# A fixed order on all engines for the attention half of an attention and MoE kernel

## The chip, the cores and the metric

The kernel runs on one core of a Trainium2 chip. The metric is the device time of one launch in microseconds (us). A core has five engines that run side by side, each working through its own queue: TensorE (PE, matrix multiplies into PSUM), VectorE (DVE), ScalarE (ACT), GpSimd (POOL, which has no access to PSUM) and SyncE (SP, which here issues the DMAs). Data lies in SBUF; PSUM has eight banks of 128 x 512 float32.

## What is computed

```
attn = softmax(causal(q @ k.T / 8))          # 2 batches x 12 heads, 448 x 64
x    = (attn @ v)                            # reshaped to 896 tokens x 768
g    = s * relu(x @ w_in)**2 + b             # 768 -> 2048
x2   = g @ w_out                             # 2048 -> 768
y    = sigmoid(x2 @ w_gate) * (x2 @ w_val)   # 768 -> 1536, twice
out  = y @ w_out2                            # 1536 -> 768
```

The divisor of the softmax is the sum of the row's exponentials plus 1e-9. The weights arrive as float64.

## The kernel before

Two heads of one batch form a pair, so there are 12 pairs, and tokens are columns: every activation is kept transposed. In the matrix products after the attention weight and activation are both split into a high and a low part, and three matmuls (`mm3`, line 104) per 128 x 128 block are added in one PSUM bank, 448 columns (one batch half) at a time. A weight block of 128 output columns is loaded as 64-bit words and turned into its two parts by `split_weights` (line 62): one DMA, an absolute value on ACT (line 70), two `tensor_scalar` (71, 74) and two `scalar_tensor_tensor` (78, 81) on DVE, the high part on ACT (87) and the low part on DVE (88). Five such blocks can be held ready (`bufs=AHEAD + 1`).

The attention of a pair has these parts. `scores` (207) makes the scores of one chunk of 128 queries for both heads, and `softmax` (199) takes each from PSUM with one DVE instruction that adds the mask, scales, and finds the row's maximum (202), then one ACT exponential that also sums the row (205). `scores3` does the last 64 queries of both heads at once. `sums` makes the reciprocals of the seven sums on DVE, copies six of them out to rows on POOL (242), and multiplies the last query chunk's probabilities by its own reciprocal on POOL (244). `transposed` (254) turns the probabilities in four groups of four 128 x 128 transposes, each group in one PSUM bank and copied out by ACT or DVE. `rows_of_sums` turns the copied reciprocals too (three transposes, line 283, one ACT copy). `values` (287) multiplies with v into one bank, and `output` (299) multiplies that by the reciprocals on DVE (304) and makes the high and the low part of x on POOL (305, 306).

The rounds run over i = 0 to 13: in round i the scores of pair i are made, the transposes of pair i - 1, and the values of pair i - 2. The first product's first four weight blocks (`AHEAD = 4`) are worked on early for the first batch: from round 8 on `fill` puts half a block (9 matmuls) in each round, two halves in rounds 12 and 13, and the rest behind the loop; then the second batch half of the four blocks follows. Seven PSUM banks go round for all of this, and one is kept for the values.

What sets the order: only PE is held to the order of the code (`manual_schedule(engines={PE})`). For DVE, ACT, POOL and SP a planner orders the instructions by priorities and costs of its own; the splits of the weight blocks are among them, and run early. After the loop the planner orders everything.

Of the kernel before, what the change touches and what calls it, by code (L numbers as in the profile page):

```python
# [15 lines left out]
P = 128  # L16
# [6 lines left out]
def body(ctx: ExitStack, tc: tile.TileContext, qk, vp, w_in, w_out, s, b, w_gate, w_val, w_out2, outT):  # L23
# [8 lines left out]
    AHEAD = 4  # L32
# [11 lines left out]
    wp = ctx.enter_context(tc.tile_pool(name="wp", bufs=AHEAD + 1))  # L44
# [17 lines left out]
    def split_weights(src, n):  # L62

        raw = wp.tile([P, U * P, 2], U32, tag="raw", name="raw", bufs=2)
        nn = n * P
        nc.sync.dma_start(out=raw[:, :nn], in_=src)
# [3 lines left out]
        nc.scalar.activation(out=f32(tt), in_=f32(high), func=AF.Abs)  # L70
        nc.vector.tensor_scalar(  # L71
            out=f32(tt), in0=f32(tt), scalar1=F64_TINY, scalar2=F64_HUGE, op0=ALU.max, op1=ALU.min,
        )
        nc.vector.tensor_scalar(  # L74
            out=tt, in0=tt, scalar1=0x07FFFFFF, scalar2=3,
            op0=ALU.bitwise_and, op1=ALU.logical_shift_left,
        )
        nc.vector.scalar_tensor_tensor(  # L78
            out=tt, in0=low, scalar=29, in1=tt, op0=ALU.logical_shift_right, op1=ALU.bitwise_or,
        )  # L80
        nc.vector.scalar_tensor_tensor(  # L81
            out=tt, in0=high, scalar=0xC0000000, in1=tt, op0=ALU.bitwise_and, op1=ALU.bitwise_or,
        )
        hi = wp.tile([P, U, P], F32R, tag="whi", name="whi")
        lo = wp.tile([P, U, P], F32R, tag="wlo", name="wlo")
        hif, lof = hi.rearrange("p k m -> p (k m)"), lo.rearrange("p k m -> p (k m)")
        nc.scalar.activation(out=hif[:, :nn], in_=f32(tt), func=AF.Copy)  # L87
        nc.vector.tensor_tensor(out=lof[:, :nn], in0=f32(tt), in1=f32(hif[:, :nn]), op=ALU.subtract)  # L88
        return hi, lo
# [16 lines left out]
    def product(src, K, x, tag):  # L106

        acc = [bank(f"acc{h}", tag) for h in range(B)]
        for unit in units(src, K):
            for h in range(B):  # L110
                mm3(acc[h], unit, K, x, h)
        return acc
# [30 lines left out]
    def first_evac(f, h, acc):  # L143
        gh, gl = at_g(f, h)
        g = ev.tile([P, S], F32, tag="e", name="g")
        nc.scalar.activation(out=g, in_=acc[:, :S], func=AF.Relu)
        nc.scalar.activation(out=g, in_=g, func=AF.Square)
        nc.vector.tensor_scalar(out=g, in0=g, scalar1=s_sb, scalar2=b_sb, op0=ALU.mult, op1=ALU.add)
        nc.scalar.activation(out=gh, in_=g, func=AF.Copy)
        lo = nc.gpsimd if f < AHEAD else nc.vector  # L150
        lo.tensor_tensor(out=gl, in0=g, in1=f32(gh), op=ALU.subtract)


    with tc.tile_pool(name="at", bufs=2) as at:
# [17 lines left out]

        all_rs = [at.tile([P, S], F32, name=f"rs{n}", bufs=1) for n in range(2)]
        for rs in all_rs:
            nc.gpsimd.memset(rs[:, NF * P:], 1.0)

# [5 lines left out]
        def load(i):  # L182

            if i >= N:
                return
            bb, hp = pairs[i]
            t = st[i]
            t["qk"] = at.tile([P, W], F32, tag="qk", name="qk", bufs=3)
            if i == 0:
                for c in range(NF):  # L190
                    both = [x[:, :2 * NF * P].rearrange("p (a b) -> p a b", a=2) for x in (t["qk"], qk[bb, hp])]
                    nc.sync.dma_start(out=both[0][:, :, c * P:(c + 1) * P], in_=both[1][:, :, c * P:(c + 1) * P])
                nc.sync.dma_start(out=t["qk"][:, 2 * NF * P:], in_=qk[bb, hp, :, 2 * NF * P:])
            else:
                nc.sync.dma_start(out=t["qk"], in_=qk[bb, hp])
            t["vt"] = at.tile([P, NQ, 2, D], F32, tag="vt", name="vt", bufs=4)
            nc.sync.dma_start(out=t["vt"], in_=vp[bb, hp])
# [9 lines left out]
        def scores(i, c):  # L207

            t = st[i]
            if "pt" not in t:  # L210
                t["pt"] = at.tile([P, 2, PO[-1] + NF * P], F32, tag="pt", name="pt", bufs=2)
                t["m"] = at.tile([P, NF * 2 + 1], F32, tag="m", name="m", bufs=3)
                t["l"] = at.tile([P, NF * 2 + 1], F32, tag="l", name="l", bufs=3)
# [9 lines left out]
        def scores3(i):  # L223

            t = st[i]
            sc = bank("sc3", "w")
            k0 = NF * P
            nc.tensor.matmul(sc[:, :S], t["qk"][:, k0 + S:], t["qk"][:, k0:k0 + S], start=True, stop=True)  # L228
            t["pt3"] = at.tile([P, S], F32, tag="pt3", name="pt3", bufs=2)
            cl = slice(NF * 2, NF * 2 + 1)  # L230
            softmax(t["pt3"], sc[:, :S], mask3, t["m"][:, cl], t["l"][:, cl])

        def sums(i):

            t = st[i]
            r = t["r"] = at.tile([P, NF * 2 + 1], F32, tag="r", name="r", bufs=3)
# [3 lines left out]
            t["rb"] = at.tile([P, NF, 2, D], F32, tag="rb", name="rb", bufs=2)  # L240
            by_chunk = r[:, :NF * 2].rearrange("p (j c o) -> p c j o", j=2, o=1)
            nc.gpsimd.tensor_copy(out=t["rb"], in_=by_chunk.to_broadcast([P, NF, 2, D]))

            nc.gpsimd.tensor_scalar(
                out=t["pt3"], in0=t["pt3"], scalar1=r[:, NF * 2:], scalar2=None, op0=ALU.mult,
            )
# [7 lines left out]
        def transposed(i):  # L254
# [16 lines left out]
            for j, copy in ((0, act), (1, dve)):  # L271
# [4 lines left out]
            put([pt3[:, k0:k0 + P] for k0 in (0, P, 2 * P, S - P)], ptT[:, :, :, NF * P:], act, "p (b a q) -> p a b q")  # L276

        def rows_of_sums(i):

            t = st[i]  # L280
            rs = bank("rs", "w")
            for c in range(NF):
                nc.tensor.transpose(rs[:, c * P:(c + 1) * P], t["rb"][:, c].rearrange("p j d -> p (j d)"), ident)  # L283
            t["rs"] = all_rs[i % 2]
            act(t["rs"][:, :NF * P], rs[:, :NF * P])
# [13 lines left out]
        def output(i):  # L299

            bb, hp = pairs[i]
            t = st[i]
            x = at.tile([P, S], F32, tag="x", name="x", bufs=2)
            nc.vector.tensor_tensor(out=x, in0=t["po"][:, :S], in1=t["rs"], op=ALU.mult)
            nc.gpsimd.tensor_copy(out=x_hi[:, hp, cols(bb)], in_=x)
            nc.gpsimd.tensor_tensor(
                out=x_lo[:, hp, cols(bb)], in0=x, in1=f32(x_hi[:, hp, cols(bb)]), op=ALU.subtract,
            )
            t.clear()

        ahead = []

        def fill(f, h, k0, k1):

            if k0 == 0:
                ahead_acc.append(bank("acc", "w"))
            wh, wl, _, _ = ahead[f][0]
            mm3(ahead_acc[-1], (wh[:, k0:k1], wl[:, k0:k1], k0, k1), KC, at_x(x_hi, x_lo), h)
            if k1 == KC:
                first_evac(f, h, ahead_acc[-1])  # L320

        ahead_acc = []

        early = [(f, k) for f in range(AHEAD) for k in range(0, KC, 3)]
        FIRST = NP + 2
        SPLIT = (5, 7, 9, 10)
        with tc.manual_schedule(engines={mybir.EngineType.PE}):
            load(0)
            load(1)
            for i in range(N + 2):  # L330
                load(i + 2)
# [3 lines left out]
                if i in SPLIT:  # L335
                    ahead.append(list(units(w_in[SPLIT.index(i)], KC)))
# [3 lines left out]
                if i >= 2:  # L340
                    values(i - 2)
                    output(i - 2)
                if i < N:
                    scores(i, 2 if i == 0 else 0)
                    scores3(i)
                    sums(i)
                if 1 <= i <= N:
                    transposed(i - 1)
                    rows_of_sums(i - 1)
                if i >= FIRST:  # L350
                    for _ in range(1 if i < N else 2):
                        f, k = early.pop(0)
                        fill(f, 0, k, k + 3)
            for f, k in early:
                fill(f, 0, k, k + 3)
            for f in range(AHEAD):
                fill(f, 1, 0, KC)

# [6 lines left out]
    for f in range(AHEAD, NF1):  # L365
        acc = product(w_in[f], KC, at_x(x_hi, x_lo), TAGS[f % 2])
# [11 lines left out]
    for d in range(KC - 1):  # L378
        acc = product(w_out[d], NF1, at_g, TAGS[d % 2])
# [24 lines left out]
    for d in range(KC):  # L404
        acc = product(w_out2[d], NF2, at_x(y_hi, y_lo), TAGS[d % 2])
# [56 lines left out]
```

## Time and profile before

| | |
|---|---|
| median of 3 runs | 596.69 us (596.21 to 597.32) |
| the profiled execution | 597.58 us, of which the trace spans 595.8 |
| PE busy | 583.8 us, 3036 matmuls |
| DVE busy | 382.3 us |
| ACT busy | 276.0 us |
| POOL busy | 59.4 us |
| values of the last pair issued on PE | up to 106.87 us |

A matmul's row is longer than the step from one matmul to the next, since they are pipelined; steps between starts are what counts on PE. DVE and ACT rows overlap their successor by 0.06 to 0.1 us.

### The profile page before, as it was taken

Reading aid. Unit: us, or ns where it says so; the run is one execution under the profiler, and the core shown is the slowest. Engines: PE = TensorE matmul, PEld = TensorE weight load, DVE = VectorE, ACT = ScalarE, POOL = GpSimd, SP = SyncE. Lnnn points to the kernel's source line nnn. Section 1 sums busy time; section 2 is a strip of 40 time slices with the busy share of each in tenths; the row PEclk is TensorE's granted clock in tenths of the full one; section 3 lists DMA queues with packets and bytes.
Section 4 is the critical chain, followed back from the end, with each engine's and each line's share of the span. In section 5 each row is a group of like instructions: output and inputs, shape, how many; then the busy total and the mean of one; then the engine's idle time right before and its main releaser. Section 6 shows DMA issues by size and latency. Waiting matters only on the chain.

```text
span 595.8 us, 7911 instructions
## 1 busy us (share of the span) xinstructions
PE 583.8 (98%) x3036; PEld 516.8 (87%) x3036; DVE 382.3 (64%) x682; ACT 276.0 (46%) x526; POOL 59.4 (10%) x69
## 2 busy tenths in 40 slices
PE   6999999999999999999999999999999999999997
PEld 3666677899999999999999999999999999999996
DVE  4699964399977776566664766666666666655000
ACT  6789786566766642332332433333333333332100
POOL 2455564320000000000000000000000000000000
PEclk9899999999999999999999999999999999999999
DMA  8366620024342332433341433333333333541000
GB/s 262 132 212 204 201 79 1 1 106 161 114 133 90 98 98 88 126 113 98 113 153 54 134 131 106 107 106 107 107 106 107 106 107 106 172 143 43 33 31 32
DMA packets 16407, 65.80 MB, mean 110 GB/s; under 512 B 2032, under 2 KB 4464, under 8 KB 16368
## 3 DMA queue, kind: packets, MB, share of 16 engines
q1 hardware_dynamic: 16368, 65.28, 33.6%
q8 instruction: 24, 0.39, 0.3%
q14 instruction: 15, 0.12, 0.1%
HBM read 62.52 MB, written 2.75 MB: 110 GB/s over the span
## 4 chain that ended last, share of the span: by engine, by line
PE 92%; DMA 3%; DVE 2%; ACT 2%; SPq 0%; issue 0%; POOL 0%; ACTq 0%; POOLq 0%
PE acc L104 83%; PE po L294 3%; PE tp L267 2%; PE sc L218 2%; DMA raw<-in_w_in 2%; PE sc L228 1%; ACT pt L205 1%; DMA qk<-in_qk 1%; DVE pt L202 1%; PE rs L283 0%; ACT wt L70 0%; DVE ptT L252 0%; DVE wlo L88 0%; DVE wt L81 0%; DVE wt L78 0%
## 5 line engine op out<-in xcount | busy, mean ns | idle before, releaser
L104 PE MATMUL acc<-x_hi,whi 128*128 128x448 f32 x480 | 175.8, 366 | 0.0
L104 PE MATMUL acc<-x_hi,wlo 128*128 128x448 f32 x480 | 175.3, 365 | 0.0
L104 PE MATMUL acc<-x_lo,whi 128*128 128x448 f32 x480 | 175.3, 365 | 0.0
L88 DVE TENSOR_TENSOR wlo<-wt,whi 128x768 fp32r<-128x768 f32 (+1 forms) x70 | 66.2, 945 | 80.7 <-ACT whi L87 80.6
L87 ACT ACTIVATE whi<-wt 128x768 fp32r<-128x768 f32 (+1 forms) x70 | 57.9, 827 | 121.7 <-PE acc L104 121.7
L104 PEld LDWEIGHTS acc<-x_hi,whi 128*128 128x128 f32 x480 | 90.2, 188 | 7.1
L104 PEld LDWEIGHTS acc<-x_hi,wlo 128*128 128x128 f32 x480 | 90.1, 188 | 7.1
L104 PEld LDWEIGHTS acc<-x_lo,whi 128*128 128x128 f32 x480 | 90.2, 188 | 7.1
L70 ACT ACTIVATE wt<-raw 128x768 f32<-128x768 f32 (+1 forms) x70 | 61.8, 883 | 35.0 <-DVE wlo L88 31.2
L81 DVE SCALAR_TENSOR_TENSOR wt<-raw,wt 128x768 uint32<-128x768 uint32 (+1 forms) x70 | 67.8, 968 | 1.1
L78 DVE SCALAR_TENSOR_TENSOR wt<-raw,wt 128x768 uint32<-128x768 uint32 (+1 forms) x70 | 65.8, 940 | 2.1
L71 DVE TENSOR_SCALAR wt<-wt 128x768 f32<-128x768 f32 (+1 forms) x70 | 39.4, 562 | 34.2 <-ACT wt L70 34.0
L104 PE MATMUL acc<-gb_hi,whi 128*128 128x448 f32 x144 | 52.6, 365 | 0.0
L104 PE MATMUL acc<-gb_hi,wlo 128*128 128x448 f32 x144 | 52.6, 365 | 0.0
L104 PE MATMUL acc<-y_hi,whi 128*128 128x448 f32 x144 | 52.6, 365 | 0.0
L104 PE MATMUL acc<-y_lo,whi 128*128 128x448 f32 x144 | 52.6, 365 | 0.0
L104 PE MATMUL acc<-y_hi,wlo 128*128 128x448 f32 x144 | 52.6, 365 | 0.0
L104 PE MATMUL acc<-gb_lo,whi 128*128 128x448 f32 x144 | 52.6, 365 | 0.0
L205 ACT ACTIVATE pt<-pt,m 128x128 f32<-128x128 f32 (+3 forms) x84 | 43.8, 524 | 13.9 <-DVE m L202 13.8
L202 DVE CUSTOM_DVE_ANT_0 pt<-sc,mask 128x128 f32<-128x128 f32 (+3 forms) x84 | 33.6, 444 | 15.9 <-PE sc L218 13.9
L74 DVE TENSOR_SCALAR wt<-wt 128x768 uint32<-128x768 uint32 (+1 forms) x70 | 40.0, 572 | 1.8
L395 ACT ACTIVATE y_hi<-y 128x448 fp32r<-128x448 f32 x24 | 13.9, 579 | 56.9 <-DVE y L394 56.9
(60 smaller groups left out, 673.7 us busy)
## 6 DMA issues: line engine op xcount, KB each, us to landing
raw<-in_w_out SPq DMA_DIRECT2D x18, 768.0 KB, 4.4
raw<-in_w_in SPq DMA_DIRECT2D x16, 768.0 KB, 4.4
raw<-in_w_gate SPq DMA_DIRECT2D x12, 768.0 KB, 4.3
raw<-in_w_val SPq DMA_DIRECT2D x12, 768.0 KB, 4.3
raw<-in_w_out SPq DMA_DIRECT2D x12, 640.0 KB, 4.0
qk<-in_qk SPq DMA_DIRECT2D x11, 480.0 KB, 5.1
vt<-in_vp SPq DMA_DIRECT2D x12, 256.0 KB, 3.8
outT<-ot SPq DMA_DIRECT2D x12, 224.0 KB, 1.9
```

The source lines that it names most:

```text
L70: nc.scalar.activation(out=f32(tt), in_=f32(high), func=AF.Abs)
L71: nc.vector.tensor_scalar(out=f32(tt), in0=f32(tt), scalar1=F64_TINY, scalar2=F64_HUGE, op0=ALU.max, op1=ALU.min,)
L74: nc.vector.tensor_scalar(out=tt, in0=tt, scalar1=0x07FFFFFF, scalar2=3, op0=ALU.bitwise_and, op1=ALU.logical_shift_left,)
L78: nc.vector.scalar_tensor_tensor(out=tt, in0=low, scalar=29, in1=tt, op0=ALU.logical_shift_right, op1=ALU.bitwise_or,)
L81: nc.vector.scalar_tensor_tensor(out=tt, in0=high, scalar=0xC0000000, in1=tt, op0=ALU.bitwise_and, op1=ALU.bitwise_or,)
L87: nc.scalar.activation(out=hif[:, :nn], in_=f32(tt), func=AF.Copy)
L88: nc.vector.tensor_tensor(out=lof[:, :nn], in0=f32(tt), in1=f32(hif[:, :nn]), op=ALU.subtract)
L104: nc.tensor.matmul(acc[:, :S], w[:, k - k0], m, start=k == 0 and i == 0, stop=k == K - 1 and i == 2)
L202: nc.vector.tensor_tensor_reduce(out=pc, in0=sc, in1=mk, scale=-SCALE, scalar=3.0e38, op0=ALU.add, op1=ALU.min, accum_out=m,)
L205: nc.scalar.activation(out=pc, in_=pc, func=AF.Exp, scale=-1.0, bias=m, accum_out=l)
L294: nc.tensor.matmul(po[j * D:(j + 1) * D, k * P:S], t["vt"][:, k, j], t["ptT"][:, j, k, k * P:], start=k == 0, stop=k == NQ - 1,)
L395: nc.scalar.activation(out=yh, in_=y, func=AF.Copy)
```

## The change

All engines are held to the code's order within the attention (`manual_schedule()` without a list). The transposes of a pair move one round further back (two rounds behind its scores), the values to three rounds behind; there are now 15 rounds. All seven probability tiles of a pair are multiplied by their reciprocals on POOL, in the round after the scores, by an instruction with two operations (times the reciprocal, times 1.0). So the transposes and the copy of the reciprocals go, the multiplication behind the values goes, and the two parts of x are taken straight from PSUM, the high one by ACT and the low one by DVE. Of the four copies behind the transposes DVE now does two and ACT two. `AHEAD` is 2: two blocks are worked on early, in rounds 12 and 13, and three more are split in the attention (`READY = 3`). The splitting of a block is cut into seven steps (load; Abs; two `tensor_scalar`; first, second `scalar_tensor_tensor`; high part; low part) that are put in by hand: one in round 2, two in each round from 3 on (one at the round's head, one ahead of the values), and more in rounds 12 to 14. Loads of v are issued later than those of q and k. Core of the diff:

```diff
-    AHEAD = 4
+    AHEAD = 2
+    READY = 3
...
-        lo = nc.gpsimd if f < AHEAD else nc.vector
-        lo.tensor_tensor(out=gl, in0=g, in1=f32(gh), op=ALU.subtract)
+        nc.vector.tensor_tensor(out=gl, in0=g, in1=f32(gh), op=ALU.subtract)
...
+        def divide(i):
+            t = st[i]
+            r = at.tile([P, NF * 2 + 1], F32, tag="r", name="r", bufs=4)
             nc.vector.tensor_scalar(out=r, in0=t["l"], scalar1=1e-9, scalar2=None, op0=ALU.add)
             nc.vector.reciprocal(out=r, in_=r)
...
+            for n, p in [
+                (j * NF + c, t["pt"][:, j, PO[c]:PO[c] + (c + 1) * P]) for c in (0, 2, 1) for j in range(2)
+            ] + [(NF * 2, t["pt3"])]:
+                nc.gpsimd.tensor_scalar(
+                    out=p, in0=p, scalar1=r[:, n:n + 1], scalar2=1.0, op0=ALU.mult, op1=ALU.mult,
+                )
...
+        def output_hi(i):
+            bb, hp = pairs[i]
+            act(x_hi[:, hp, cols(bb)], st[i]["po"][:, :S])
+        def output_lo(i):
+            bb, hp = pairs[i]
+            nc.vector.tensor_tensor(
+                out=x_lo[:, hp, cols(bb)], in0=st[i]["po"][:, :S], in1=f32(x_hi[:, hp, cols(bb)]), op=ALU.subtract,
+            )
...
-        with tc.manual_schedule(engines={mybir.EngineType.PE}):
+        with tc.manual_schedule():
+            load_qk(0)
+            load_qk(1)
+            for i in range(N + 3):
+                load_qk(i + 2)
+                load_v(i - 1)
...
+                on(i - 1, divide)
+                if i >= 2:
+                    step()
                 if i < N:
                     for c in (0, 1) if i == 0 else (2, 1):
                         scores(i, c)
+                if i >= 3:
+                    step()
+                on(i - 3, values)
+                on(i - 3, output_hi)
                 if i < N:
                     scores(i, 2 if i == 0 else 0)
+                on(i - 3, output_lo)
+                on(i, scores3)
+                tail = i >= N
+                if i == N:
+                    fill(0, 0, 0, KC)
+                    step(3)
+                t = turned(i - 2) if 0 <= i - 2 < N else iter(())
+                next(t, None)          # first group of transposes, ACT copy
+                on(i, softmax3)
+                next(t, None)          # three more groups: DVE, ACT, DVE copies
+                if i == N + 1:
+                    fill(1, 0, 0, KC)
+                if tail:
+                    step(4)
             for f in range(AHEAD):
                 fill(f, 1, 0, KC)
+                step(5)
```

The comments behind the two `next` lines are added here.

## Rows read from the trace of the kernel before

**Rows 1.** The page's busy time by engine, and two windows (busy by engine, clock).

```profile
PE 583.8 (98%) x3036; PEld 516.8 (87%) x3036; DVE 382.3 (64%) x682; ACT 276.0 (46%) x526; POOL 59.4 (10%) x69
...
20.00:70.00 50.00, 47.71 (x334) 32.48 (x331) 48.13 (x146) 46.12 (x132) 26.86 (x27) 1.00 0.58 181
...
106.87:595.00 488.13, 485.45 (x2398) 449.51 (x2394) 305.19 (x431) 192.49 (x289) 8.78 (x8) 1.00 0.31 102
```

**Rows 2.** PE in order of time, one round (start, length), and behind the last values.

```profile
80.32 1.35 PE L218 MATMUL sc<-qk 64*128 64x384 f32 x8
81.60 1.95 PE L294 MATMUL po<-ptT,vt 128*64 128x448 f32 x16
83.48 0.49 PE L218 MATMUL sc<-qk 64*128 64x128 f32 x4
...
84.75 1.91 PE L267 MATMUL tp<-ident,pt 128*128 128x128 f32 x16
86.50 0.49 PE L283 MATMUL rs<-ident,rb 128*128 128x128 f32 x3
...
106.87 0.47 PE L104 MATMUL acc<-x_hi,whi 128*128 128x448 f32 x1
```

**Rows 3.** DVE in order of time: single instructions of the attention.

```profile
18.52 0.56 DVE L202 CUSTOM_DVE_ANT_0 pt<-sc,mask 128x384 f32<-128x384 f32 x1 [4.23 <-PE sc L218]
...
66.06 0.95 DVE L88 TENSOR_TENSOR wlo<-wt,whi 128x768 fp32r<-128x768 f32 x1
...
79.52 0.17 DVE L237 TENSOR_SCALAR r<-l 128x7 f32<-128x7 f32 x1 [0.72 <-ACT pt L205]
...
89.69 0.56 DVE L202 CUSTOM_DVE_ANT_0 pt<-sc,mask 128x384 f32<-128x384 f32 x1 [2.43 <-PE sc L218]
...
92.12 0.62 DVE L304 TENSOR_TENSOR x<-po,rs 128x448 f32<-128x448 f32 x1 [0.69 <-ACT pt L205]
...
93.49 0.62 DVE L202 CUSTOM_DVE_ANT_0 pt<-sc,mask 128x448 f32<-128x448 f32 x1 [0.33 <-POOL x_hi L305]
...
94.69 0.69 DVE L252 COPY ptT<-tp 128x512 f32<-128x512 f32 x1 [0.57 <-PE tp L267]
```

**Rows 4.** ACT: the page's group of all exponentials, then rows in order of time.

```profile
L205 ACT ACTIVATE pt<-pt,m 128x128 f32<-128x128 f32 (+3 forms) x84 | 43.8, 524 | 13.9 <-DVE m L202 13.8
```

**Rows 5.** ACT in order of time: single instructions of the attention.

```profile
9.04 0.67 ACT L205 ACTIVATE pt<-pt,m 128x448 f32<-128x448 f32 x1 [0.67 <-DVE m L202]
...
59.91 0.95 ACT L70 ACTIVATE wt<-raw 128x768 f32<-128x768 f32 x1
...
78.26 0.58 ACT L249 ACTIVATE ptT<-tp 128x512 f32<-128x512 f32 x1
78.74 0.66 ACT L205 ACTIVATE pt<-pt,m 128x448 f32<-128x448 f32 x1
...
90.30 0.61 ACT L205 ACTIVATE pt<-pt,m 128x384 f32<-128x384 f32 x1 [2.30 <-DVE m L202]
...
92.40 0.18 ACT L205 ACTIVATION_READ_ACCUMULATOR pt<-pt,m 128x1 f32 x1
```

**Rows 6.** Evacuation of an early block: ACT, DVE and POOL in order of time.

```profile
105.09 0.55 ACT L146 ACTIVATE g<-acc 128x448 f32<-128x448 f32 x1 [3.06 <-PE acc L104]
...
106.28 0.51 DVE L148 TENSOR_SCALAR g<-g,s_sb,b_sb 128x448 f32<-128x448 f32 x1 [4.97 <-ACT g L147]
...
107.48 1.15 POOL L151 TENSOR_TENSOR ga_lo<-g,ga_hi 128x448 fp32r<-128x448 f32 x1 [4.93 <-ACT ga_hi L149]
```

**Rows 7.** Windows at the start: busy PE, PEld, DVE, ACT, POOL, granted clock, DMA.

```profile
13.00:16.00 3.00, 0.38 (x3) 0.38 (x4) 0.68 (x3) 2.06 (x7) 1.91 (x2) 1.00 1.01 415
...
18.00:19.00 1.00, 1.00 (x6) 0.34 (x2) 0.47 (x1) 0.00 (x0) 0.00 (x0) 0.50 0.07 31
```

**Rows 8.** POOL groups of 0 to 110 us: busy us, mean ns of one.

```profile
L244 POOL TENSOR_SCALAR pt<-pt,r 128x448 f32<-128x448 f32 x12 | 17.6, 1463 | 0.0
...
L305 POOL CAST x_hi<-x 128x448 fp32r<-128x448 f32 x12 | 6.7, 557 | 15.4 <-DVE x L304 15.3
```

More of the change, by code (lines that the diff above doesn't have):

```diff
@@ L77, in split_weights @@
         )
+        yield
         nc.vector.scalar_tensor_tensor(
@@ L87, in split_weights @@
         nc.scalar.activation(out=hif[:, :nn], in_=f32(tt), func=AF.Copy)
+        yield
         nc.vector.tensor_tensor(out=lof[:, :nn], in0=f32(tt), in1=f32(hif[:, :nn]), op=ALU.subtract)
-        return hi, lo
+        out += [hi, lo]
+    def split_weights(src, n):
+        out = []
+        for _ in split_steps(load_words(src, n), n, out):
+            pass
+        return out
     def units(src, K):
@@ L104, in mm3, with product @@
                 nc.tensor.matmul(acc[:, :S], w[:, k - k0], m, start=k == 0 and i == 0, stop=k == K - 1 and i == 2)
-    def product(src, K, x, tag):
+    def product(parts, K, x, tag):
         acc = [bank(f"acc{h}", tag) for h in range(B)]
-        for unit in units(src, K):
+        for unit in parts:
             for h in range(B):
@@ L180, in body, with load_qk @@
         st = [{} for _ in pairs]
-        def load(i):
+        def load_qk(i):
             if i >= N:
@@ L311, in body @@
-        ahead = []
+            act(x_hi[:, hp, cols(bb)], st[i]["po"][:, :S])
[3 more added lines that the diff above has]
+                out=x_lo[:, hp, cols(bb)], in0=st[i]["po"][:, :S], in1=f32(x_hi[:, hp, cols(bb)]), op=ALU.subtract,
+            )
+            st[i].clear()
+        split = [[] for _ in range(AHEAD + READY)]
+        acc = {}
         def fill(f, h, k0, k1):
             if k0 == 0:
-                ahead_acc.append(bank("acc", "w"))
-            wh, wl, _, _ = ahead[f][0]
-            mm3(ahead_acc[-1], (wh[:, k0:k1], wl[:, k0:k1], k0, k1), KC, at_x(x_hi, x_lo), h)
+                acc[f] = bank("acc", "w")
+            wh, wl = split[f]
+            mm3(acc[f], (wh[:, k0:k1], wl[:, k0:k1], k0, k1), KC, at_x(x_hi, x_lo), h)
@@ L319, in fill, with splits @@
             if k1 == KC:
[L320 to L326, printed above, removed]
-        with tc.manual_schedule(engines={mybir.EngineType.PE}):
[L328 to L331, printed above, removed]
+                first_evac(f, h, acc[f])
+        def splits():
+            for f in range(AHEAD + READY):
+                raw = load_words(w_in[f], KC)
+                yield
+                yield from split_steps(raw, KC, split[f])
+                yield
@@ L332, in body, with step, on @@
+        steps = splits()
+        def step(n=1):
+            for _ in range(n):
+                next(steps, None)
+        def on(i, *what):
+            if 0 <= i < N:
+                for w in what:
+                    w(i)
+        with tc.manual_schedule():
[4 more added lines that the diff above has]
+                load_v(i - 1)
                 if i == 0:
@@ L339, in body @@
                         scores(i, c)
-                if i >= 2:
-                    values(i - 2)
-                    output(i - 2)
+                if i >= 3:
+                    step()
+                on(i - 3, values)
+                on(i - 3, output_hi)
                 if i < N:
                     scores(i, 2 if i == 0 else 0)
[L345 to L355, printed above, removed]
+                on(i - 3, output_lo)
[12 more added lines that the diff above has]
+                    step(4)
             for f in range(AHEAD):
                 fill(f, 1, 0, KC)
+                step(5)
+            for _ in steps:
+                pass
     gb = ctx.enter_context(tc.tile_pool(name="gb", bufs=1))
@@ L365, in body @@
     for f in range(AHEAD, NF1):
-        acc = product(w_in[f], KC, at_x(x_hi, x_lo), TAGS[f % 2])
+        ready = [(*split[f], 0, KC)] if f < AHEAD + READY else units(w_in[f], KC)
+        acc = product(ready, KC, at_x(x_hi, x_lo), TAGS[f % 2])
         for h in range(B):
```

80 lines of the change are left out of this document (30 added, 50 removed).

## The prediction

> **What bounds the kernel now.** First the page's busy times and the windows. From 106.87 us to the end PE works without a gap at full clock, 2398 matmuls in 485.45 us, 0.203 us each [rows 1]. The matmuls there are a fixed amount that the change doesn't touch, so a time saved or lost ahead of it passes through one to one, and the sum below is only about when PE gets into this stream. Between 20 and 70 us DVE is busy 48.13 of 50 us and ACT 46.12: the splits of seven weight blocks lie on DVE beside the softmax, and PE waits [rows 1]. From round 8 on the early blocks fill PE.
>
> PE's order shows one round: 80.32 to 86.50 us is 6.18 us for scores (1.28 and 1.27), values (1.88) and 16 transposes (1.75); the reciprocals' transposes come behind that [rows 2].
>
> Before, 54 matmuls of the early blocks (nine each in rounds 8 to 11, 18 in round 12) are done when the last values end at 106.87 us, so 52 at 106.46. I look for the time at which the changed kernel goes on without a gap with 52 done, and compare.
>
> **The change, part by part.**
>
> *What goes.* Three transposes a pair (under 0.5 us on PE [rows 2]), an ACT copy, the multiplication on DVE (0.62) and two POOL instructions for x. None is worth its length by itself: what counts is the chain of a round in its new order.
>
> *The chain of a round.* In code order DVE has: two small instructions for the reciprocals (they wait for the last exponential of the pair before), a split step, four mask instructions, a split step, two more, the low part of x (which waits for ACT's high part), the seventh mask instruction, two copies of 512 columns. ACT has: split step, four exponentials, split step, the high part of x, two exponentials, a copy, the seventh exponential, a copy. The high part waits for the values on PE; behind it wait ACT's last three exponentials, and through them the next round's reciprocals. Starts, since rows overlap: first mask instruction to first exponential 0.61 (89.69 to 90.30 [rows 3, 5]); four exponentials 2.19 (to 92.40, and the read behind it 0.1 [rows 5]); high part 0.55 with its handover (the copy of 512 took 0.48, 78.26 to 78.74 [rows 5]); low part 0.53 and seventh mask 0.54 (0.62 each less the overlap), two copies 1.2 (0.69 each) and the two small ones 0.3 (0.17 the first) [rows 3]. Sum 5.92 us; PE's part of the round is 6.18 and lies beside it.
>
> Steps of a split add to this chain in two places only. A DVE step at the head stands ahead of the first mask instruction: 0.87 (the low part's row, 0.95 less overlap [rows 3]), or 1.0 for the two tensor_scalars. An ACT step ahead of the high part adds 0.8 (0.95 for Abs [rows 5]). The rest falls into DVE's wait for the high part or ACT's wait for the first mask. Counting seven steps a block, two a round: DVE steps at the heads of rounds 4, 7, 8, 9 and 11 (4 x 0.87 + 1.0 = 4.5), ACT steps ahead of the high part in rounds 6 and 8 (1.6).
>
> *The start.* The first pair is as before, its last exponential at 9.04 us [rows 5]. From there the reciprocals start 0.78 later (78.74 to 79.52 [rows 3, 5]) and the next first mask 0.3 behind: 10.1. A pair's seven exponentials take 3.65 us (43.8/12 [rows 4]), 2.98 to the start of the seventh. So the first mask of pair 2 starts at 10.1 + 0.61 + 2.98 + 1.08 = 14.8, of pair 3 (one ACT copy more, 0.48) at 19.95. Before, pair 2 started at 18.52, behind 4.23 us of waiting for PE [rows 3]: 3.7 us are won here.
>
> *Rounds 3 to 11.* The first mask of pair 11 starts at 19.95 + 8 x 5.92 + 4.5 + 1.6 + 0.3 (round 3, where PE's 6.18 is longer) = 73.7. POOL's long run of divisions starts right behind the reciprocals, beside the DVE steps at the head. No row shows those two together; 0 if DVE has the lead each time, 2.8 if each of five steps waits for one POOL instruction as long as the cast (0.56 [rows 8]); a gain is excluded, since POOL can only take away. I take 0.3, as DVE's step issues first: 74.0.
>
> *Rounds 12 to 14.* Here the order costs. From 74.0, the last copies of round 11 end 5.65 later, values (1.9) and the first early block (18 x 0.203 and 0.2) bring PE to F = +11.5. Its evacuation stands in code ahead of the transposes' copies and a split's steps. It takes 1.2 from the first ACT instruction to the one on DVE and 2.4 to the last subtraction [rows 6], which moves from POOL to DVE (0.53). So DVE is free at F + 3.0, Abs ends at 3.2, two tensor_scalars take 1.0, the two copies 1.2, and PE, done with its transposes at F + 1.75, gets its values at F + 5.6: 3.85 us idle. Then values, transposes and the second block (1.9 + 1.75 + 3.85): G = F + 13.1; the copies of pair 11 are ahead of this evacuation, so the last values follow at once. But the parts of pair 11's x stand behind evacuation (3.0), two tensor_scalars (1.0), two steps (1.75), the high part of a weight block (0.85), its low part (0.9) and their own length: the low part is there at G + 8.4, while PE needs it at G + 5.1 for the sixth slice: 3.3 idle. PE goes on with 52 done at 74.0 + 11.5 + 13.1 + 8.4 = 107.0.
>
> The Trainium skill, page "PSUM — Partial Sum Buffer", section "Engine vs sequencer instructions", states that the queues of ScalarE, VectorE and GpSimdE are strict first in, first out, which speaks against this part of the change; by that rule both idle times stand, without it PE would be through 7.15 us earlier (the third rival).
>
> *The clock.* Before, PE was busy 0.38 us of 13 to 16 us, and in 18 to 19 us the granted clock was 0.50 (1.2 of 2.4 GHz) [rows 7]. A stretch of about 3 us at half clock costs some 1.6. Two idle times could cost 0 to 3.2 in all; PE comes into these from full work, which the row did not, so I take one: 1.6.
>
> *At no cost.* POOL, if its divisions are short (below): the transposes come a round and more behind the divisions. Loads: SP's order has q and k two rounds ahead of use, v two rounds, and each weight block more than a step ahead; SP waits only for buffers read a round before. If that cover went, a 768 KB load would be seen at the Abs. After the loop three blocks lie ready (21.8 us of PE work) for the next split to come, so the stream has no gap; the gb tiles wait for the attention's space, which is free before their first writer comes.
>
> **Sum.** 107.0 + 1.6 - 106.46 = +2.1 us on the profiled 597.58, so 599.7; the median lies 0.89 lower, 598.8. Own range 596 to 602 (clock 0 to 3.2, POOL beside DVE 0 to 2.8).
>
> *The price of a division.* The instruction with two operations isn't in the trace. Ends: the cast, 0.557 for 448 columns, and the one-operation row, 1.404 at its usual, 1.463 on average [rows 8]. A pair has 1984 columns: 2.5 or 6.5 us, with seven starts perhaps 3.1 or 6.7. The nearest row is the dear one, and even 6.5 is inside a mean round of 6.8 (54.05/8 over rounds 3 to 10). So the sum doesn't hang on it until 7.0: twelve pairs from 10.1 us must end by the last transposes, F + 9 = 94.5. The cheap end gives no more than the sum above, as POOL is off the path there.
>
> The Trainium skill, page "GPSIMD Engine Reference", section 4.1, calls one-input instructions on GpSimd roughly line rate. The cast bears that out and the one-operation multiplication does not; by the page POOL would need 2.5 us a pair and the second rival falls, by the row it stays.
>
> **Rivals.**
>
> 1. PE sets the rounds (not slower). If the head steps were hidden, rounds 3 to 10 take 6.18 each: first mask of pair 11 at 19.95 + 49.4 = 69.4, 4.6 earlier: 594.2. For it: ACT's own work in a round, 3.65 + 0.45 + 2 x 0.48 and some 0.45 of splits, is 5.5, below PE's 6.18. Against: the reciprocals and the step really stand ahead of the mask in one queue.
>
> 2. POOL becomes the bound (slower). The divisions cost the one-operation row (6.2 a pair by its usual 1.404), and the 14 DVE instructions of splits in rounds 3 to 11 hold POOL besides, each by nothing to its length of 0.87, up to 1.4 a round: 6.2 to 7.6 a pair, and 7.9 by the mean row. I price it at 7.5. Then pair 11 is divided at 10.1 + 12 x 7.5 = 100.1 and its transposes come 5.6 late: 604.4. It decides from 7.0 a pair on. For it: the multiplication's row, which rose from 1.404 to 1.463 in the mean by waits. Against: the cast's.
>
> 3. The order isn't held on DVE and ACT as written, or copies get ahead of the evacuations: the idle 7.15 and the clock's 1.6 go: 590.0. For it: the trace of before has another order and can't exclude it. Against: the call names no engine, so it binds all.
>
> **Chances.** Forecast 0.45 (slower 0.31, same 0.10, faster 0.04), first rival 0.25 (faster 0.21, same 0.04), second 0.22 (slower 0.19, same 0.03), third 0.08 (faster). Sums: faster 0.33, same 0.17, slower 0.50; a difference within 0.2% (1.2 us) is what a measurement can't tell from none. The range 591 to 606 leaves out most of the third rival and the far end of the second.
>
> **What would show it.** Right: mask instructions of pair 3 near 20 us and of pair 11 near 74; rounds that are longer where a DVE step stands at the head; two PE gaps of 3 to 4 us between 85 and 107 us, the first ended by a DVE copy, the second by the low part of x; the unbroken stream from some 107 us. Wrong: POOL rows above 1.4 us for 448 columns and PE waiting for POOL in each round (rival 2), rounds of 6.2 (rival 1), copies of round 12 ahead of the evacuation (rival 3). A gap in the later stream would break the premise.

## The result and the profile after

The changed kernel took 602.41, 604.06 and 604.36 us against 596.21 to 597.32 before: ratio 1.0113, 95% interval 1.0088 to 1.0139, some 6.7 us slower. Forecast was 598.8 (591 to 606), so the side was right and the size too small by about 5 us; the median, 604.06, lies inside the range but beyond the end of what the sum itself allowed (596 to 602). Executions in which the whole matmul stream ran 2% slower at full granted clock (in e1's profile 2131 matmuls in the 440 us from 130 us on, in the changed kernel's 2172), 8 to 12 us longer in all, are left out; only the ratios of e1 and e4 hold one each, 615.87 and 610.63, and of the profiles of e1, e6 and e9, which are of such executions, only the attention is read.

The profiled execution took 602.41 us with a span of 600.6, against a span of 595.8 before: 4.8 us to account for, where +2.1 was forecast. The page's busy times by engine, and the shares of the chain that ended last:

```profile
PE 580.5 (97%) x3000; PEld 515.3 (86%) x3000; DVE 390.2 (65%) x702; ACT 272.2 (45%) x514; POOL 50.5 (8%) x95
...
PE 84%; DVE 7%; ACT 5%; DMA 2%; issue 1%; SPq 0%; ACTq 0%; DVEq 0%
```

The same line of the page of before:

```profile
PE 92%; DMA 3%; DVE 2%; ACT 2%; SPq 0%; issue 0%; POOL 0%; ACTq 0%; POOLq 0%
```

PE has 36 matmuls less than before (three a pair) and POOL 9 us less work [rows 1]; neither made it faster. In the chain DVE and ACT now have 12%, where they had 2% each before: more of the time ahead of the stream is theirs. Windows of the changed kernel (busy of PE, PEld, DVE, ACT, POOL, then granted clock, DMA share, GB/s):

```profile
20.00:70.00 50.00, 46.77 (x338) 31.86 (x334) 42.19 (x150) 40.90 (x129) 29.29 (x52) 1.00 0.41 134
...
90.00:95.00 5.00, 2.76 (x10) 1.43 (x12) 4.02 (x7) 1.69 (x4) 0.00 (x0) 0.74 0.00 0
...
110.00:115.00 5.00, 5.00 (x18) 4.55 (x19) 4.49 (x7) 3.66 (x6) 0.00 (x0) 0.72 0.21 86
...
113.00:595.00 482.00, 482.00 (x2380) 446.82 (x2379) 305.46 (x438) 192.22 (x287) 0.00 (x0) 1.00 0.32 103
```

The last row is the fixed stream: 482.00/2380 = 0.203 us a matmul, as before [rows 1]. So the premise held, and the whole difference arises ahead of 113 us. The second and third rows are the places where the granted clock fell. DVE in order of time, the first mask instructions of pairs 6 and 7, and then the stretch of the early blocks:

```profile
38.13 0.56 DVE L214 CUSTOM_DVE_ANT_0 pt<-sc,mask 128x384 f32<-128x384 f32 x1
...
47.78 0.54 DVE L214 CUSTOM_DVE_ANT_0 pt<-sc,mask 128x384 f32<-128x384 f32 x1
...
87.84 0.51 DVE L163 TENSOR_SCALAR g<-g,s_sb,b_sb 128x448 f32<-128x448 f32 x1 [3.83 <-ACT g L162]
...
89.78 0.56 DVE L76 TENSOR_SCALAR wt<-wt 128x768 f32<-128x768 f32 x1 [0.16 <-ACT wt L74]
90.38 0.56 DVE L79 TENSOR_SCALAR wt<-wt 128x768 uint32<-128x768 uint32 x1
90.85 1.28 DVE L265 COPY ptT<-tp 128x512 f32<-128x512 f32 x2
...
102.69 0.51 DVE L163 TENSOR_SCALAR g<-g,s_sb,b_sb 128x448 f32<-128x448 f32 x1
...
108.43 0.96 DVE L97 TENSOR_TENSOR wlo<-wt,whi 128x768 fp32r<-128x768 f32 x1 [0.91 <-ACT whi L95]
109.31 0.62 DVE L311 TENSOR_TENSOR x_lo<-po,x_hi 128x448 fp32r<-128x448 f32 x1
```

The first masks of pairs 3 to 11 start at 19.16, 26.18, 32.18, 38.13, 47.78, 54.53, 62.03, 67.97 and 74.99 us. So rounds with no split step in the chain last 5.94 to 6.00 us, those with a step in it 6.75 to 7.50, and one, round 6, lasts 9.65. In that round, ACT in order of time shows:

```profile
40.83 0.19 ACT L217 ACTIVATION_READ_ACCUMULATOR pt<-pt,m 128x1 f32 x1
42.73 0.91 ACT L74 ACTIVATE wt<-raw 128x768 f32<-128x768 f32 x1 [1.72 <-DMA raw<-in_w_in]
43.55 0.53 ACT L262 ACTIVATE x_hi<-po 128x448 fp32r<-128x448 f32 x1
```

SP issued that load at 36.27 us, in the same round's code; ACT stood 1.72 us for it, and the high part of x, the last exponentials and the next round's reciprocals stood behind. PE at the end of the attention:

```profile
86.45 1.91 PE L280 MATMUL tp<-ident,pt 128*128 128x128 f32 x16
92.24 3.61 PE L299 MATMUL po<-ptT,vt 128*64 128x448 f32 x16 [3.88 <-issue]
95.78 1.97 PE L280 MATMUL tp<-ident,pt 128*128 128x128 f32 x16
...
101.39 1.95 PE L299 MATMUL po<-ptT,vt 128*64 128x448 f32 x16
...
108.88 0.47 PE L119 MATMUL acc<-x_hi,whi 128*128 128x448 f32 x1 [2.30 <-ACT x_hi L262]
109.98 0.74 PE L119 MATMUL acc<-x_lo,whi 128*128 128x448 f32 x1 [0.62 <-DVE x_lo L311]
110.52 0.58 PE L119 MATMUL acc<-x_hi,wlo 128*128 128x448 f32 x1
...
113.00 0.36 PE L119 MATMUL acc<-x_hi,whi 128*128 128x448 f32 x1
```

The two gaps stand where they were forecast: 3.88 us ended by DVE's copies (the row names no releaser; the copies at 90.85 to 92.1 end it), then 2.30 and 0.62 for the parts of the last pair's x. The length of the values behind the first (3.61, and 1.95 at full clock) and the matmul step of 0.37 us from 110 to 113 us (0.20 later) are the clock at half.

So the 4.8 us, against the forecast: +2.1 as forecast; -0.8 because pair 3 came at 19.16 and not 19.95 (a favour of this one execution: in e2, e3 and e10, which have the same code up to there, it came at 19.65 to 19.93); +1.8 in rounds 3 to 10 (55.83 us against 54.05), which is the wait for the load; +0.4 from pair 11 to PE going on with 52 matmuls done (109.98 - 74.99 = 35.0, forecast 33.0 and 1.6 for the clock); +1.2 for the second stretch at half clock (nine matmuls in 3.0 us from 109.98, 1.8 at full). Sum 4.7.

The executions without a profile are up to 2 us longer than the profiled one, at about the same mean clock (0.990 and 0.994 against 0.994). What differs in them no trace shows; that stays open. Two things do differ between profiles of the same code: the start of pair 3, as said, and the wait for the load, which was 1.72 us here and 1.88, 1.92 and 4.03 us in e2, e10 and e3.

### The profile page after: what moved, and what is told of

It reads as the page before. It is cut to its first block, busy times and chain, and to the rows that moved or that the text cites. A ratio compares the mean times of both kernels' runs of the same rounds, so it can differ in the third digit from the quotient of the medians.

```text
span 600.6 us, 7898 instructions
## 1 busy us (share of the span) xinstructions
PE 580.5 (97%) x3000; PEld 515.3 (86%) x3000; DVE 390.2 (65%) x702; ACT 272.2 (45%) x514; POOL 50.5 (8%) x95
## 4 chain that ended last, share of the span: by engine, by line
PE 84%; DVE 7%; ACT 5%; DMA 2%; issue 1%; SPq 0%; ACTq 0%; DVEq 0%
PE acc L119 82%; ACT pt L217 3%; DVE pt L214 2%; DMA raw<-in_w_in 2%; DVE ptT L265 2%; PE po L299 1%; DVE wt L84 1%; PE sc L230 1%; DVE wt L88 1%; PE sc L240 1%; DVE wt L76 1%; DVE wt L79 0%; DMA qk<-in_qk 0%; ACT x_hi L262 0%; PE tp L280 0%
## 5 line engine op out<-in xcount | busy, mean ns | idle before, releaser
L84 DVE SCALAR_TENSOR_TENSOR wt<-raw,wt 128x768 uint32<-128x768 uint32 (+1 forms) x70 | 65.5, 935 | 2.1
L88 DVE SCALAR_TENSOR_TENSOR wt<-raw,wt 128x768 uint32<-128x768 uint32 (+1 forms) x70 | 65.2, 932 | 1.2
L119 PE MATMUL acc<-gb_hi,wlo 128*128 128x448 f32 x168 | 61.4, 365 | 0.0
L119 PE MATMUL acc<-gb_lo,whi 128*128 128x448 f32 x168 | 61.4, 365 | 0.0
L119 PE MATMUL acc<-gb_hi,whi 128*128 128x448 f32 x168 | 61.4, 365 | 0.0
L257 POOL TENSOR_SCALAR pt<-pt,r 128x128 f32<-128x128 f32 (+3 forms) x84 | 47.5, 584 | 34.1 <-DVE r L253 32.4
L79 DVE TENSOR_SCALAR wt<-wt 128x768 uint32<-128x768 uint32 (+1 forms) x70 | 38.7, 553 | 1.9
```

Source lines behind the costliest of these rows:

```text
L79: nc.vector.tensor_scalar(out=tt, in0=tt, scalar1=0x07FFFFFF, scalar2=3, op0=ALU.bitwise_and, op1=ALU.logical_shift_left,)
L84: nc.vector.scalar_tensor_tensor(out=tt, in0=low, scalar=29, in1=tt, op0=ALU.logical_shift_right, op1=ALU.bitwise_or,)
L88: nc.vector.scalar_tensor_tensor(out=tt, in0=high, scalar=0xC0000000, in1=tt, op0=ALU.bitwise_and, op1=ALU.bitwise_or,)
L119: nc.tensor.matmul(acc[:, :S], w[:, k - k0], m, start=k == 0 and i == 0, stop=k == K - 1 and i == 2)
L257: nc.gpsimd.tensor_scalar(out=p, in0=p, scalar1=r[:, n:n + 1], scalar2=1.0, op0=ALU.mult, op1=ALU.mult,)
```

## Experiments

The theory: the order written out by hand costs, in three places. A split's work and the evacuations stand ahead of copies and x that PE needs (two gaps); a step's load stands too near to its use (round 6); steps at the heads of rounds lengthen the chain. The rivals are that POOL's divisions set the pace, and that PE sets the rounds anyway.

**e1: the division with one operation.**

```diff
-  out=p, in0=p, scalar1=r[:, n:n + 1], scalar2=1.0, op0=ALU.mult, op1=ALU.mult,
+  out=p, in0=p, scalar1=r[:, n:n + 1], scalar2=None, op0=ALU.mult,
```

> The changed kernel, but each division on POOL is one operation again (times the reciprocal, without the second factor 1.0). Theory A (POOL lies off the path, the chain of DVE and ACT and the end of the attention set the time): with two operations a pair's divisions took 3.4 to 4.6 us of rounds of 6 to 7; at the price of the one-operation row of before, 1.4 us for 448 columns, they would take 6.2 to 7.6 and just fit or come up to 4 us late at the end: 604 to 608. Theory B (the second operation costs nothing or less than nothing because the one-operation form costs the same with this operand): rows of 0.64 us for 448 columns as now, 604 +- 1.5. Theory C (POOL bound already): rows grow and the time grows by ten pairs times their growth, 625 or more.

607.25 and 607.43 us, some 10.6 over before (1.018 by these two; the ratio with the third time is 1.0231 [1.0176, 1.0286]). POOL's group for the widest rows (busy, mean ns), first in the changed kernel and then in e1:

```profile
L257 POOL TENSOR_SCALAR pt<-pt,r 128x448 f32<-128x448 f32 x12 | 7.6, 636 | 0.0
```

```profile
L257 POOL TENSOR_SCALAR pt<-pt,r 128x448 f32<-128x448 f32 x12 | 17.9, 1494 | 0.0
```

POOL in order of time, the last pair in the changed kernel and then all pairs in e1:

```profile
81.20 4.13 POOL L257 TENSOR_SCALAR pt<-pt,r 128x128 f32<-128x128 f32 x7 [2.20 <-DVE r L253]
```

```profile
10.39 87.06 POOL L257 TENSOR_SCALAR pt<-pt,r 128x128 f32<-128x128 f32 x84 [6.69 <-DVE r L253]
```

84 divisions without a gap, 87.06/12 = 7.25 us a pair: with one operation POOL never rests, and rounds 3 to 10 last 7.19 us in the mean (20.31 to 77.81), 6.98 in the changed kernel. POOL is the bound then, some 3 us beyond the changed kernel by these two times. With two operations a pair takes 3.4 to 4.6 us, and POOL stands idle 1.2 to 5.2 us ahead of each. The second rival holds for the dear price only, and the changed kernel doesn't pay it.

The Trainium skill, page "GPSIMD Engine Reference", section 4.1 (Engine selection), calls one-input instructions on GpSimd roughly line rate. At 448 columns the traces agree for the form with two operations (636 ns beside the cast's 557 [rows 8]) and not for that with one (1494).

**e2: round 12's copies ahead of the first evacuation and its steps.**

```diff
-  fill(0, 0, 0, KC)
-  step(3)
+  fill(0, 0, 0, KC, evac=False)
...
   next(t, None)
+  if i == N:
+      first_evac(0, 0, acc[0])
+      step(3)
```

> The changed kernel, with the evacuation of the first early block and the three split steps behind it put behind the copies of round 12's transposes in the code; PE's order is the same. Theory A (the 4 us without a matmul from 88 to 92 us come from the order of DVE's and ACT's queues): this idle time falls from about 4 us to under 1, and with it the fall of the granted clock behind it (the values took 3.61 us there, 1.95 elsewhere): 604.2 - 3.3 - 1.7 = about 599, with the second idle time (106 to 109 us) as it was. Rival (PE would wait there anyway, for POOL's divisions of the last pair or for a PSUM bank): the idle time stays within 1 us of what it was, 603 to 605.

602.22 to 605.07 us, ratio 1.0116 [1.0093, 1.0139]: no gain that shows, a miss. PE in order of time:

```profile
90.13 1.95 PE L299 MATMUL po<-ptT,vt 128*64 128x448 f32 x16 [0.83 <-ACT g L161]
...
99.77 1.95 PE L299 MATMUL po<-ptT,vt 128*64 128x448 f32 x16 [2.08 <-ACT g L161]
...
108.75 0.74 PE L119 MATMUL acc<-x_hi,whi 128*128 128x448 f32 x1 [3.79 <-ACT x_hi L262]
109.85 0.74 PE L119 MATMUL acc<-x_lo,whi 128*128 128x448 f32 x1 [0.35 <-DVE x_lo L311]
```

The first gap is 0.83 and the clock stays up there, but PE stands 2.08 us ahead of the last values and 3.79 and 0.35 us for the last pair's x, 7.05 us in all against 6.80: DVE and ACT have the same list of work ahead of that x, and the idle time moves to where the list ends. Counted from pair 11's first mask (75.92), PE goes on only 1.1 us sooner than in the changed kernel (33.93 us and 34.99), and the clock, 0.50 in all of 110 to 115 us, takes that back: to the end it is 525.9 us (601.8 - 75.92), in the changed kernel 525.6.

**e3: the second evacuation and four steps behind the last pair's x.**

```diff
-  fill(1, 0, 0, KC)
-  if tail:
+  fill(1, 0, 0, KC, evac=False)
+  if i == N + 2:
+      first_evac(1, 0, acc[1])
+  if i == N or i == N + 2:
       step(4)
```

> The changed kernel, with the evacuation of the second early block and the four split steps of round 13 put behind the two parts of the last pair's x. Theory A (the 2.3 and 0.6 us of waiting from 106.4 to 110 us and the half clock from 110 to 113 us come from the queue order): x's high part follows the last values at once, both waits go, and the clock stays: 604.2 - 3.2 - 1.4 = about 599.5, the first idle time as it was. Rival (the clock falls because of the first idle time, or the values' bank is late): waits gone but the clock still low, 601 to 603.

Ten times from 597.51 to 599.74, median 598.34, ratio 1.0033 [1.0017, 1.0049]: 5.7 us less than the changed kernel's median. From the first mask of pair 11 to the end it takes 519.4 us (597.7 - 78.34), the changed kernel 525.6. ACT at the Abs of round 6, then PE, in order of time:

```profile
45.60 0.89 ACT L74 ACTIVATE wt<-raw 128x768 f32<-128x768 f32 x1 [4.03 <-DMA raw<-in_w_in]
```

```profile
48.22 0.70 PE L230 MATMUL sc<-qk 64*128 64x256 f32 x4 [3.41 <-ACT ptT L262]
49.38 3.61 PE L299 MATMUL po<-ptT,vt 128*64 128x448 f32 x16 [0.45 <-DVE ptT L265]
...
95.66 1.95 PE L299 MATMUL po<-ptT,vt 128*64 128x448 f32 x16 [3.88 <-issue]
```

The second gap is gone. The first is as long as ever, 3.88, but this time the values behind it run at full clock, while those at 49.38, behind 3.41 us of waiting, run at half. A gap of this length may cost the clock or not; only where the granted clock was low does a trace say that it did. So of the 6.2 us, 2.9 are the second gap, 1.2 the second fall of the clock and some 1.7 the first fall, which did not come here; 0.4 stays open. The wait at 45.60 is for the same load as in the changed kernel, issued at 36.82 us: ACT stood 4.03 us for it and not 1.72, and round 6 lasts 11.95 us here.

**e4: each weight block's load a block earlier.**

```diff
+  raws = [load_words(w_in[0], KC)]
   for f in range(AHEAD + READY):
-      raw = load_words(w_in[f], KC)
+      if f + 1 < AHEAD + READY:
+          raws.append(load_words(w_in[f + 1], KC))
       yield
-      yield from split_steps(raw, KC, split[f])
+      yield from split_steps(raws[f], KC, split[f])
```

> The changed kernel, with each weight block's load issued one block (seven steps) earlier; the split steps stay where they are. Theory A (in round 6 the Abs of the second block stands behind its own load's step in the same round and ACT waited 1.72 us for that DMA, all on the chain): round 6 to 7 falls from 9.65 to about 7.8 us, 604.2 - 1.8 = about 602.4. Rival (the wait is swallowed by slack between PE and the chain): round 6 is shorter, round 7 and 8 longer by as much, 604 +- 0.7.

601.72, 602.69 and 602.91 us, 1.4 below the changed kernel in the median, though the times overlap (602.41 to 604.36), so they alone don't show a gain. The ratio, with the fourth time, is 1.0136 [1.0088, 1.0184]; the median of the three is 1.010 of before. In round 6 ACT no longer waits for the load:

```profile
41.57 0.92 ACT L74 ACTIVATE wt<-raw 128x768 f32<-128x768 f32 x1
```

The round takes 7.85 us (38.77 to 46.62) and not 9.65, which shows the cause of that round's length. Part of it is given back: from pair 11 to the end this profile takes 527.3 us against 525.6, with the clock at 0.50 in all of 90 to 95 us.

**e5: only PE's order fixed, the rest left to the planner.**

```diff
-  with tc.manual_schedule():
+  with tc.manual_schedule(engines={mybir.EngineType.PE}):
```

> The changed kernel with only PE held to the code's order (as before); DVE, ACT, POOL and SP are ordered by the planner again. It splits the change into its order by hand and the rest (deeper pipeline, divisions on POOL, two blocks). Theory A (hand order costs at the end, through steps ahead of the last pair's x and copies behind an evacuation): the idle times of rounds 12 to 14 go, but the planner puts splits early and rounds 3 to 8 grow to 7.5 to 8 us as before; the first mask of pair 11 comes near 80 us instead of 75: 596 to 600. Rival (the deeper pipeline or the fewer early blocks cost by themselves): 603 to 606 with the loss in the tail still there, then from PE's lack of work.

Twelve times from 594.53 to 597.3, median 595.34, ratio 0.9979 [0.9963, 0.9994]. Its rounds last 6.6 to 7.4 us, in sum about as long as the fixed ones (56.66 and 55.83 us), but pair 3 comes at 17.03, and the gaps at the end are shorter. PE in order of time:

```profile
81.12 2.71 PE L299 MATMUL po<-ptT,vt 128*64 128x448 f32 x16 [2.44 <-ACT pt L217]
...
91.33 1.95 PE L299 MATMUL po<-ptT,vt 128*64 128x448 f32 x16 [1.04 <-ACT ga_hi L164]
```

From pair 11 to the end it is 519.6 us (593.3 - 73.69). So what the change does to the work itself (no transposes of reciprocals, divisions ahead of the transposes, two blocks) makes the kernel no slower; the order written out for the other engines is what costs 8 us. The run gives DVE, ACT, POOL and SP back together, so it doesn't part the order of the loads from that of the steps; e4 and e7 do.

**e6: e4, and both steps of a round ahead of the values, none at the head.**

```diff
-  if i >= 2:
+  if i == 2 or i >= N:
       step()
...
-      step()
+      step(2 if i < N else 1)
```

> The kernel of e4_load_early (602.4 in comparable executions), with both split steps of rounds 3 to 11 put ahead of the values, none at a round's head. Theory A (a DVE step at the head adds its length to the chain of the round; behind the fourth mask it falls into DVE's wait for the high part of x): rounds 4, 7, 8, 9, 11 fall by 0.9 to 1.0 us, towards PE's 6.2, unless two DVE steps of 1.75 together, or an ACT step that moves ahead of the high part (0.8, in rounds 5 and 10 too), take it back; the first mask of pair 11 moves from 73.8 to 70.5 to 72.5, 599 to 601. Rival (PE or its waits for the copies set the rounds already): no earlier than 73.3, 602 to 603.

605.21, 605.69 and 606.49 us, ratio 1.0151 [1.012, 1.0182]: a miss, 3 us more than e4. Rounds 3 to 10 last 7.80, 6.99, 7.54, 6.77, 7.34, 7.23, 5.95 and 7.81 us, so pair 11 comes at 77.42 where e4 has 73.83. The only round with a DVE step and no ACT step there, 5.95, is as short as one with none: one such step fits in DVE's wait for the high part, two don't (6.99 and 7.34), and ACT's steps in that place stand ahead of the high part itself. e8 has the same rounds and shows the same lengths.

**e7: e4, both evacuations behind what PE waits for, and the steps of rounds 13 and 14 behind the last pair's x.**

```diff
-  if i >= 2:
+  if 2 <= i <= N:
...
-  if i >= 3:
+  if 3 <= i <= N:
...
-  fill(0, 0, 0, KC)
-  step(3)
+  fill(0, 0, 0, KC, evac=False)
...
+  if i == N:
+      first_evac(0, 0, acc[0])
   if i == N + 1:
-      fill(1, 0, 0, KC)
-  if tail:
+      fill(1, 0, 0, KC, evac=False)
+  if i == N + 2:
+      first_evac(1, 0, acc[1])
       step(4)
```

> The kernel of e4_load_early (602.4), and all split steps of rounds 13 and 14 and those behind the early blocks put behind the two parts of the last pair's x; both evacuations too come behind the copies or that x. Theory A (what counts is how much work of splits and evacuations stands ahead of the last pair's x in DVE's and ACT's queues; putting a part of it elsewhere ahead of it, as in e2_copies_first, only moves the idle time): both idle times fall to under 1 us, and the half clock with them: 602.4 - 3.3 - 2.9 - 1.7 - 1.4 = about 593, under the time before. Rival 1 (the splits of blocks 3 and 4 then come late for the stream): a new PE wait of several us between 115 and 130 us, 596 to 600. Rival 2 (some other wait holds PE in the tail): idle time stays, 598 to 600.

590.88 to 592.06 us, median 591.74, ratio 0.9914 [0.9893, 0.9935]: faster than both kernels. The only idle times of PE from 76 to 112 us:

```profile
79.37 1.97 PE L299 MATMUL po<-ptT,vt 128*64 128x448 f32 x16 [1.59 <-ACT ptT L262]
...
87.77 1.95 PE L299 MATMUL po<-ptT,vt 128*64 128x448 f32 x16 [0.83 <-ACT g L161]
```

The granted clock is 1.00 throughout. From pair 11 to the end it takes 516.1 us, 9.5 less than the changed kernel: 3.05 and 2.92 of gaps, 1.66 and 1.2 of clock, which makes 8.8; the other 0.7 stays open.

**e8: e6 and e7 together.**

```diff
-  if 2 <= i <= N:
+  if i == 2 or i == N:
...
-      step()
+      step(2 if i < N else 1)
```

(against e7)

> e6_steps_in_wait and e7_steps_last together: about 593 less what e6 gains over e4 (1.5 to 3): 590 to 591.5. If the two overlap, because PE's own work in rounds and tail is the bound then, 592 to 593.

595.55 to 596.58 us, ratio 0.9993 [0.998, 1.0005], 4.5 over e7: a miss for e6's reason. Its rounds 3 to 10 last 7.82, 7.00, 7.54, 6.78, 7.35, 7.22, 5.94 and 7.83 us, as in e6, and pair 11 comes at 76.64, 3.1 later than in e7. From there to the end it is 517.3 us (593.9 - 76.64), 1.2 more than in e7, which these rounds don't explain.

**e9: e7, with loads and ACT's steps at the heads and one DVE step ahead of the values.**

```diff
+  kinds = "LADDDAD" * (AHEAD + READY)
...
-  if 2 <= i <= N:
+  if i == 2:
       step()
+  if 3 <= i <= N:
+      step_if("LA")
...
-      step()
+      step_if("D")
```

(against e7; L is a load, A a step on ACT, D one on DVE; a step is taken only if it is of a kind named)

> The kernel of e7_steps_last (591.7), with the split steps of rounds 3 to 12 placed by engine: ACT's steps and loads at a round's head, and at most one DVE step a round ahead of the values. Theory A (in the rounds so far a lone ACT step at the head and a lone DVE step ahead of the values cost nothing, 5.94 to 6.00 us, while a DVE step at the head costs its 0.83 to 1.05): every round falls to 6.0 to 6.3, where PE's own 6.18 sets it, the first mask of pair 11 moves from 73.6 to 69.5 to 70.5, and the time by as much: 587.5 to 589, under everything so far. Rival (fewer steps are done in the rounds, so blocks 2 to 4 come late for the stream): a PE wait behind the early blocks, 590 to 594.

588.32 to 589.46 us, median 588.72, ratio 0.9876 [0.9853, 0.99]: the fastest. DVE's first masks of pairs 10 and 11:

```profile
63.90 0.56 DVE L214 CUSTOM_DVE_ANT_0 pt<-sc,mask 128x384 f32<-128x384 f32 x1
...
70.17 0.56 DVE L214 CUSTOM_DVE_ANT_0 pt<-sc,mask 128x384 f32<-128x384 f32 x1
```

All rounds from pair 3 to 11 last 6.23 to 6.28 us, and PE is busy 49.83 of the 50 us from 20 to 70: here PE sets the rounds, as the first rival said. (In this execution the stream takes 0.206 us a matmul and not 0.203, so PE's own 6.18 would be some 6.3; that is an estimate.) One wait is new, 0.73 us at 110.38 for the low part of a weight block.

**e10: the changed kernel, with PE kept busy in both gaps.** 34 and 25 transposes that nobody reads are added.

```diff
+  if i == N:
+      keep_busy(34)
...
-  for f in range(AHEAD):
-      fill(f, 1, 0, KC)
-      step(5)
+  fill(0, 1, 0, 5)
+  keep_busy(25)
+  fill(0, 1, 5, KC)
+  step(5)
+  fill(1, 1, 0, KC)
+  step(5)
```

> The changed kernel with transposes of the identity, whose result nobody reads, put into PE's two idle times: 34 behind round 12's transposes, 25 ahead of the last slice of the first early block's second half. DVE's and ACT's work is unchanged, so the waits for it stay. Theory A (the half clock behind each idle time comes of the idling and costs 1.4 to 1.7 us each): the granted clock stays 1.00 from 85 to 115 us and the time falls by some 3: 601 to 601.5. Rival (the clock falls for another reason, or its price is hidden by the same waits): the time stays at 603.5 to 604.5.

601.68 to 602.41 us, ratio 1.0101 [1.0077, 1.0125], which overlaps the changed kernel's. Windows of the profiled execution:

```profile
90.00:95.00 5.00, 4.79 (x44) 3.92 (x42) 4.58 (x7) 1.69 (x4) 0.00 (x0) 1.00 0.00 0
...
110.00:115.00 5.00, 4.37 (x21) 3.81 (x22) 4.54 (x8) 3.93 (x6) 0.00 (x0) 1.00 0.34 138
```

The clock holds at 1.00 at both places, so its falls there go with the idle times, though e3 shows that not every such idle time brings one (the mean clock of e10's executions is 0.994 to 1.000). But from pair 11 to the end this saves only 1.0 us (600.4 - 75.80 = 524.6, against 525.6). The values of pair 11 start 1.6 us sooner after pair 11's mask (24.78 and not 26.40), and yet x_lo doesn't (34.54 and 34.32). Why, ACT and DVE show; here in e10:

```profile
99.74 0.89 ACT L74 ACTIVATE wt<-raw 128x768 f32<-128x768 f32 x1 [1.79 <-DMA raw<-in_w_in]
```

```profile
102.85 0.96 DVE L88 SCALAR_TENSOR_TENSOR wt<-raw,wt 128x768 uint32<-128x768 uint32 x1
103.73 0.51 DVE L163 TENSOR_SCALAR g<-g,s_sb,b_sb 128x448 f32<-128x448 f32 x1
```

and DVE in the changed kernel:

```profile
101.78 0.96 DVE L88 SCALAR_TENSOR_TENSOR wt<-raw,wt 128x768 uint32<-128x768 uint32 x1
102.69 0.51 DVE L163 TENSOR_SCALAR g<-g,s_sb,b_sb 128x448 f32<-128x448 f32 x1
```

By the count of steps this Abs belongs to a split from behind the loop, which the planner puts between the fixed instructions. Four DVE instructions follow it (100.67 to 103.8), and the second evacuation's part on DVE stands behind them, at 103.73 us, 3.15 after the values began. In the changed kernel the same four run from 99.59 to 102.7, just as long as the slow clock holds PE up. So of these two, only the later one counts: 1.7 us for the first fall of the clock, or 1.9 for the split (in e10 ACT's part of the evacuation was ready at 101.85). The 1.0 us that e10 saves is the second fall's 1.2 less the 0.2 by which x_lo comes later. No run takes that split out of e10, so this is read from the rows and not tested.

## Why the prediction was right in its side and small in its size

- **The place.** That everything is decided ahead of an unbroken stream of 0.203 us a matmul held to the last digit.
- **The chain.** 5.92 us was worked out; 5.94, 5.95 and 6.00 were measured in the rounds without a step in it, and a DVE step at the head adds 0.8 to 1.1 (6.75, 7.02). The start was 0.8 better than worked out, by luck: the same code started within 0.3 of it in e2, e3 and e10. The first rival's bound, PE's own round, isn't met in this kernel (rounds of 5.94 to 9.65) but in e9.
- **The failing step: loads at no cost.** "each weight block more than a step ahead" was counted in steps, not in time. In round 6 load and Abs are the two steps of one round, at its head and ahead of the values. The text gave what would follow if the cover went ("seen at the Abs") but not that round's length. It cost 1.72 us in the profile (4.03 in e3's), and e4, which takes it away, brings the round from 9.65 to 7.85; without the load the sum's own terms gave 7.7 for it.
- **The gaps.** 3.85 was worked out and 3.88 measured; 3.3 was worked out and 2.92 measured. e2 and e3 show that the list of work ahead of the last x, not any one idle time, is what costs: closing the first gap alone gave nothing, moving the list of the second 5.7 us (some 1.7 of it a fall of the clock that did not come), both together with e4 12 us. The Trainium skill, page "PSUM — Partial Sum Buffer", section "Engine vs sequencer instructions", has the queues as strict first in, first out; the trace agrees, as two copies whose input was ready at about 88.4 us ran at 90.85, behind an evacuation and two tensor_scalars.
- **The mis-sized term: the clock.** One fall of 1.6 was taken out of 0 to 3.2. Two came, 1.66 and 1.2, together 2.9, near the far end of what was given. That the first cost its length is in part luck: without it the split from behind the loop, which the sum didn't have, would have cost about as much (e10).
- **POOL.** The sum was said not to hang on its price up to 7.0 us a pair. At 3.4 to 4.6 it doesn't; at e1's 7.25 it does. The nearest row, one operation, was the wrong one for this form.
- **The third rival**, an order not held, falls: copies ran behind the evacuation. But the binding is not complete, since instructions from outside the block were put in between.

## What to carry to other kernels

Where an order is fixed by hand, count for each engine all that stands ahead of the instruction the bottleneck waits for, up to the point where the bottleneck no longer waits; closing one gap moves the idle time to the end of that list (e2), and moving work behind it gives it back (e3, e7). Place side work by engine, into that engine's own wait and no more than fits (e6 against e9). A load and its first use should be rounds apart, not steps.

## What the runs showed of the hardware

On POOL a tensor_scalar over 448 columns took 636 ns with two operations and 1494 with one, for the same product. Dummy transposes kept the granted clock at 1.00 where 3.88 us of idling had dropped it to half (e10); the same idle time left it at 1.00 in e3. One 768 KB load, issued at the same place of the same code, kept ACT waiting 1.72 to 1.92 us in three profiles and 4.03 us in a fourth.
